# An earlier V load, bias copies on another queue and P V one head closer, in attention followed by a feed-forward block

## The chip, the cores and the metric

One Trainium2 chip, one core. Time is device time in microseconds of one launch. Each time is the median of several executions; the profile is one execution of its own.

## The reference, cut to what matters

```python
scores = q @ k^T / sqrt(64)                       # 8 batches x 8 heads, 576 positions
bias   = -(cum[..., :, None] - cum[..., None, :]) # cum = cumsum(max(s, 0))
scores = where(causal, -1e9, scores + minimum(bias, 0))
attn   = softmax(scores)
x      = (attn @ v).transpose(0, 2, 1, 3).reshape(4608, 512)
out    = (silu(x @ w_gate) * (x @ w_val)) @ w_out # 512 -> 1536 -> 512, float32
```

## The kernel before, in words

Attention runs head by head, 64 heads (`bh`), eight to a batch. Heads are grouped in sixteen blocks of four (`hb`). For a block, k and q are loaded in float32 (`load_one`, L112), cast to bfloat16 (`cast_one`, L191 and L193), transposed on TensorE (`pe_transpose`, L224; later blocks through a DMA) and copied into `KQ[hb % 2]` (`pe_out`, L237 and L239). The bias is not added by an engine: four rows of `KQ` beside the 64 of a head hold the cumulated s, as high and low parts (`HL`), so that the score product adds it. `aug(hb, ...)` (L178) copies these rows with four small DMAs, one for each head of the block, on the queues that it is given. `KQ[1]` needs memsets first, one of them at L505.

For one head `score_piece` makes the scores in four chunks (L268), ScalarE takes the exponential into `pt` (L276), and GpSimd masks the first and the last chunk (L280, L285). `av_piece` (L301) multiplies `pt` with V; V has 65 columns, the last all ones, so the row sums come along. `av_out` (L316, L317) divides by them on VectorE and leaves a bfloat16 tile `ot` for two heads; `x_pe` (L333) transposes that tile for the feed-forward part.

V of a batch is loaded in five chunks of up to 128 positions (`load_v`, L129, on SyncE's queue), into one buffer, in runs of 64 floats, and cast chunk by chunk (`cast_v`, L136). The first V is cast on GpSimd within the second head. Feed-forward weights are loaded and cast by DMAs that GpSimd issues (`w_load`, L250).

`attn_items` sets the order of the attention's work by a count `kk`. In the first batch P V of a head stands `lag` = 3 heads behind its scores, later 1. Where the first batch ends, `kk` runs on for four counts without scores, and then the second batch starts. `ffn_items` makes one tile of 512 rows: twelve times a gate product (`pg`, L453), a tanh, a value product (`pv`, L466) and two VectorE operations, and then the output products (`py`, L477). The main loop first runs `attn_items` to the end of the first batch (`start`) and then mixes it into the feed-forward items by `lo` and `hi`. Each engine and each queue works in the order in which its instructions were written. PSUM: three banks for scores (`scp`), one for P V (`avp`), four shared by transposes and feed-forward (`mp`).

Order of SyncE's queue at the start: s, k and q of blocks 0 and 1, bias copies of block 1, the first V, bias copies of block 2, k and q of block 2; then, behind the first batch's last scores, bias copies of block 3, the second V, k and q of blocks 3 and 4.

Of the kernel before, what the change touches and what calls it, by code (L numbers as in the profile page):

```python
# [12 lines left out]
FP32 = mybir.dt.float32  # L13
# [6 lines left out]
def kernel(  # L20
# [11 lines left out]
    nc = tc.nc  # L32
    PSUM = bass.MemoryType.PSUM

    B, H, S, D = q.shape
    NT, DM = out.shape
    DF = moe_w_gate.shape[1]
    BH = B * H
    NCH = 5
# [24 lines left out]
    def pt_col(tj, bi):  # L64
        if tj == bi:
            return DIAG_OFF[tj]
        return OFF_OFF[tj] + 128 * (bi - tj - 1)
# [11 lines left out]
    avp = ctx.enter_context(tc.tile_pool(name="avp", bufs=1, space=PSUM))  # L79
    mp = ctx.enter_context(tc.tile_pool(name="mp", bufs=4, space=PSUM))  # L80
# [23 lines left out]
    with tc.manual_schedule():  # L104
# [3 lines left out]
        def load_one(hb, name, rs=(0, NR)):  # L108
            b, g = divmod(hb, 2)
            if rs[0] == 0:  # L110
                loaded[name, hb] = raw.tile([128, NR, J, D], FP32, tag="raw" + name, name="raw" + name)
            nc.sync.dma_start(  # L112
                loaded[name, hb][:, rs[0] : rs[1], :, :].rearrange("x r j d -> x r (j d)"),
                SRC[name][0][b, g * HB + 2 * rs[0] : g * HB + 2 * rs[1], :, :].rearrange(
                    "(r e) (p j) d -> (e p) r (j d)", e=2, j=J
                ),
            )

        def load_qk(hb):
            load_one(hb, "k")  # L120
            load_one(hb, "q")

        def load_v(b, cs):
            if 0 in cs:
                loaded["v", b] = raw.tile([128, NCH, H, D], FP32, tag="rawv", bufs=1, name="rawv")
            t = loaded["v", b]
            for c in cs:
                n = 128 if c < 4 else TAIL
                nc.sync.dma_start(  # L129
                    t[0:n, c, :, :],  # L130
                    v[b, :, c * 128 : c * 128 + n, :].rearrange("h p d -> p h d"),
                )
# [5 lines left out]
        nc.sync.dma_start(s_sb, s.rearrange("b h n -> (b h) n"))  # L138
        load_qk(0)
        load_qk(1)  # L140

        ONES2 = 1.0019378662109375
        NEGS2 = -1.0058441162109375

        def aug_rows(i, r):
            r0 = 64 * (1 - r)
            return KQ[i][r][r0 : r0 + 64, :, :].bitcast(FP32)
# [26 lines left out]
        def aug(hb, engs):  # L174
            for hh in range(HB):
                r, e = divmod(hh, 2)
                r0 = 64 * (1 - r)
                engs[hh].dma_start(  # L178
                    KQ[hb % 2][r][r0 : r0 + 4, :, e * S : (e + 1) * S],
                    HL[hb * HB + hh : hb * HB + hh + 1, :, :, :],  # L180
                )

        SP4 = [nc.sync] * 4
# [3 lines left out]
        def cast_one(hb, name, eng):  # L187
            cts[name, hb] = cp.tile([128, J, NR, D], BF16, tag="c" + name, bufs=2, name="c" + name)
            dst = cts[name, hb].rearrange("x j r d -> x r j d")
            if eng is nc.scalar:  # L190
                nc.scalar.copy(dst, loaded[name, hb])  # L191
            else:
                eng.tensor_copy(dst, loaded[name, hb])  # L193
# [25 lines left out]
        def pe_transpose(hb, name, g):  # L219
            j0, j1 = JG[g]  # L220
            ps = mp.tile([128, j1 - j0, 128], BF16, tag="m", name="tps")
            ct = cts[name, hb]
            for j in range(j0, j1):
                nc.tensor.transpose(  # L224
                    ps[:, j - j0, :], ct[:, j].rearrange("x r d -> x (r d)"), ident
                )
            tps[name, g] = ps

        def pe_out(hb, name, g, r, eng):
            j0, j1 = JG[g]  # L230
            kq = SRC[name][1]
            dst = KQ[hb % 2][r][64 * r : 64 * r + 64, kq, 0 : NR * S].rearrange(
                "a (x j) -> a x j", j=J
            )[:, :, j0:j1]
            srcp = tps[name, g][64 * r : 64 * r + 64].rearrange("a j x -> a x j")
            if eng is nc.scalar:
                nc.scalar.copy(dst, srcp)  # L237
            else:
                eng.tensor_copy(dst, srcp)  # L239
# [50 lines left out]
        avs = {}  # L290

        def av_piece(bh, bis):
            b, h = divmod(bh, H)
            if bis[0] == 0:
                avs[bh] = avp.tile([128, NCH * (D + 1)], FP32, tag="av", name="av")
            av = avs[bh]
            pt = pts[bh]
            for bi in bis:
                for tj in range(bi + 1):
                    c0 = pt_col(tj, bi)  # L300
                    nc.tensor.matmul(  # L301
                        av[:, bi * (D + 1) : (bi + 1) * (D + 1)],
                        pt[:, c0 : c0 + 128],
                        VT[b % 2][:, tj, h, :],
                        start=(tj == 0),
                        stop=(tj == bi),
                    )
# [91 lines left out]
                        cast_v(bn, 4, nc.gpsimd)  # L399

        def attn_items():
            for kk in range(BH + 6):
                first = kk < H + 4
                bh = kk if first else kk - 4
                lag = 3 if first else 1
                b_lo, b_hi = (0, H) if first else (H, BH)
                h, step = divmod(bh, HB)
                if not first and step == 0 and 2 <= h < NPE:
                    if h > 3:
                        aug(h, SP4)  # L410
                    cast_one(h, "k", nc.gpsimd)
                    cast_one(h, "q", nc.gpsimd)
                    yield kk + 0.01
                    yield kk + 0.02
                    for g in range(2):
                        for nm in ("k", "q"):
                            pe_transpose(h, nm, g)
                            pe_out(h, nm, g, 0, nc.vector)
                            pe_out(h, nm, g, 1, nc.scalar)
                            yield kk + 0.03 + 0.02 * g  # L420
                if first and bh == H:
                    aug(3, SP4)
                    load_v(1, range(5))
                    load_qk(3)
                    load_qk(4)
                if bh < b_hi:
                    for ci in range(4):
                        score_piece(bh, ci)
                        if ci == 1:
                            side(h, step)  # L430
                        yield kk + 0.1 + ci / 8
                x = bh - lag - 1
                if b_lo <= x < b_hi and x % 2 == 1:
                    x_pe(x // 2)
                    yield kk + 0.5
                p = bh - lag
                if b_lo <= p < b_hi:
                    av_piece(p, (0, 1, 2))
                    yield kk + 0.6
                    av_piece(p, (3,))  # L440
                    yield kk + 0.7
                    av_piece(p, (4,))
                    av_out(p)
                    yield kk + 0.8
# [46 lines left out]
        def init_vt(i):  # L491
            nc.gpsimd.memset(VT[i][:, :, :, D : D + 1], 1.0)
            nc.gpsimd.memset(VT[i][64:128, 4, :, 0:D], 0.0)

        cast_one(0, "k", nc.scalar)
        cast_one(0, "q", nc.vector)
        aug(0, [nc.gpsimd] * 4)
        for nm, eng in (("k", nc.scalar), ("q", nc.vector)):
# [3 lines left out]
        for nm, eng in (("k", nc.scalar), ("q", nc.vector)):  # L502
            for g in range(2):
                pe_out(0, nm, g, 1, eng)
        nc.vector.memset(aug_rows(1, 1)[:, 0, :], 0.0)  # L505
        aug(1, SP4)
        load_v(0, range(5))
        init_vt(0)
        cast_one(1, "k", nc.vector)
        cast_one(1, "q", nc.vector)  # L510

        at = attn_items()
        state = {"pos": -1.0}

        def pump(upto):
            while state["pos"] < upto:
                try:
                    state["pos"] = next(at)
                except StopIteration:
                    state["pos"] = 1e9  # L520

        LAG = 1.65
        start = H + 3.45
        pump(start)
        hook = {
            21: [lambda: load_qk(5)],
        }
        for tt in range(NTT):
            lo = start if tt == 0 else H * (tt + 1) + 4 + LAG
            hi = min(H * (tt + 2) + 4 + LAG, BH + 6)  # L530
            span = 36
            n0 = 6 if tt == 0 else 0
            n = 0
            for _ in ffn_items(tt):
                n += 1
                for f in hook.pop(n, ()):
                    f()
                pump(lo + (hi - lo) * min(1.0, max(0, n - n0) / (span - n0)))
# [31 lines left out]
```

## Time and profile before

| | us |
|---|---|
| median of 3 executions | 427.64 (427.57 to 428.98) |
| the profiled execution | 429.72 |
| its span, first to last instruction | 428.0 |
| TensorE busy in it | 387.8 (91%) |
| VectorE, ScalarE, GpSimd busy | 251.3, 212.1, 124.2 |

Busy shares are means over the whole span. The first tenth of the kernel is different from the rest: there the attention of the first batch runs alone, and the feed-forward part begins only after it.

### The profile page before, as it was taken

The numbers are of one execution on the slowest core, as the hardware profiler recorded it, in microseconds if no ns is written. First come the engines' busy times: TensorE is split into PE (matmuls) and PEld (weight loads), VectorE is DVE, ScalarE is ACT, GpSimd is POOL, SyncE is SP. The second block draws the span as 40 slices with busy tenths as digits, with TensorE's granted clock in tenths as the row PEclk, the third lists the DMA queues.
The fourth block names the chain that finished last, engine by engine and source line by source line (L and its number), as shares of the span: only waits on it lengthen the run. The fifth ranks groups of instructions, "written<-read, shape, count | busy, mean of one in ns | idle before, by whom it ended". The sixth has DMA issues, their size and how long they took to land.

```text
span 428.0 us, 7940 instructions
## 1 busy us (share of the span) xinstructions
PE 387.8 (91%) x3029; PEld 214.8 (50%) x3082; DVE 251.3 (59%) x494; ACT 212.1 (50%) x421; POOL 124.2 (29%) x220
## 2 busy tenths in 40 slices
PE   2618779798999999999999999999999999999996
PEld 1416435454555555555555555555555554444442
DVE  7804466544688358836873686369636751871760
ACT  7506156555665555556555655555545552322321
POOL 5528023363416231623252235223411110000000
PEclk9957689898999999999999999999999999999999
DMA  6599979636493579447836774573320001002002
GB/s 238 108 176 231 186 237 182 221 102 182 141 239 91 167 185 219 112 163 184 204 99 200 176 188 112 187 188 81 94 78 26 2 13 70 17 2 99 0 2 98
DMA packets 85255, 56.71 MB, mean 132 GB/s; under 512 B 65456, under 2 KB 69520, under 8 KB 85216
## 3 DMA queue, kind: packets, MB, share of 16 engines
q1 hardware_dynamic: 81408, 51.44, 42.9%
q0 software_dynamic: 3808, 4.76, 6.8%
q8 instruction: 24, 0.39, 0.4%
q14 instruction: 15, 0.12, 0.1%
HBM read 37.90 MB, written 15.93 MB: 126 GB/s over the span
## 4 chain that ended last, share of the span: by engine, by line
PE 87%; DMA 5%; DVE 4%; issue 1%; SPq 1%; ACT 1%; POOL 0%; ACTq 0%
PE pg L453 22%; PE py L477 22%; PE pv L466 22%; PE sc L268 10%; PE av L301 8%; DMA rawv<-in_v_dram 3%; PE xps L333 3%; DVE kq L239 3%; DMA rawq<-in_q_dram 1%; DVE ot L317 1%; ACT pt L276 1%; SPq L129 0%; PE tps L224 0%; DVE ht L471 0%; SPq L178 0%
## 5 line engine op out<-in xcount | busy, mean ns | idle before, releaser
L276 ACT ACTIVATE pt<-sc 128x512 bf16<-128x512 f32 (+1 forms) x256 | 117.4, 505 | 66.5 <-PE sc L268 53.8
L460 DVE SCALAR_TENSOR_TENSOR pp<-th,pg 128x512 bf16<-128x512 bf16 x108 | 74.2, 687 | 66.0 <-ACT th L458 65.5
L453 PE MATMUL pg<-xt,wg 128*128 128x512 bf16 x416 | 111.4, 384 | 1.3 <-issue 0.5
L466 PE MATMUL pv<-xt,wv 128*128 128x512 bf16 x411 | 110.5, 384 | 1.2 <-issue 0.2
L458 ACT ACTIVATE th<-pg 128x512 bf16<-128x512 f32 x108 | 64.5, 597 | 91.3 <-PE pg L453 91.3
L477 PE MATMUL py<-wo,ht 128*128 128x512 bf16 x416 | 103.9, 382 | 0.9
L268 PE MATMUL sc<-kq 128*128 128x128 bf16 (+4 forms) x576 | 77.8, 250 | 8.3 <-DVE kq L239 5.5
L280 POOL TENSOR_SCALAR_AFFINE_SELECT pt<-pt 128x512 bf16<-128x512 bf16 x64 | 42.5, 665 | 146.1 <-ACT pt L276 143.7
L471 DVE TENSOR_TENSOR ht<-pp,pv 128x512 bf16<-128x512 bf16 x108 | 73.9, 685 | 9.1 <-PE pv L466 1.5
L268 PEld LDWEIGHTS <-kq 128*128 128x128 bf16 x576 | 47.6, 102 | 44.3 <-issue 6.1
L301 PE MATMUL av<-vt,pt 128*128 128x65 bf16 x960 | 51.6, 197 | 12.1 <-POOL vt L136 9.3
L301 PEld LDWEIGHTS <-pt 128*128 128x128 bf16 x960 | 42.4, 100 | 30.9 <-issue 12.5
L453 PEld LDWEIGHTS <-wg 128*128 128x128 bf16 x432 | 38.7, 99 | 36.9 <-issue 1.9
L466 PEld LDWEIGHTS <-wv 128*128 128x128 bf16 x432 | 38.9, 99 | 35.9 <-issue 1.9
L477 PEld LDWEIGHTS <-ht 128*128 128x128 bf16 x432 | 38.3, 98 | 35.4 <-issue 0.6
L485 ACT ACTIVATE ysb<-py 128x512 f32<-128x512 f32 x36 | 21.5, 597 | 44.5 <-PE py L477 42.4
L316 DVE RECIPROCAL rc<-av 128x5 f32<-128x5 f32 x64 | 12.2, 191 | 47.7 <-PE av L301 47.5
L285 POOL TENSOR_SCALAR_AFFINE_SELECT pt<-pt 128x64 bf16<-128x64 bf16 x64 | 15.4, 240 | 66.5 <-ACT pt L276 64.8
L317 DVE TENSOR_TENSOR ot<-av,rc 128x320 bf16<-128x320 f32 x64 | 31.5, 492 | 2.2
L337 DVE COPY xt<-xps 128x64 bf16<-128x64 bf16 (+7 forms) x32 | 9.8, 305 | 35.2 <-PE xps L333 35.2
L136 POOL CAST vt<-rawv 128x512 bf16<-128x512 f32 (+1 forms) x40 | 25.9, 673 | 9.5 <-DMA rawv<-in_v_dram 9.5
L333 PE MATMUL xps<-ident,ot 128*128 128x128 bf16 (+1 forms) x160 | 17.1, 220 | 1.6 <-DVE ot L317 1.6
(44 smaller groups left out, 152.9 us busy)
## 6 DMA issues: line engine op xcount, KB each, us to landing
rawk<-in_k_dram SPq DMA_DIRECT2D x16, 576.0 KB
rawq<-in_q_dram SPq DMA_DIRECT2D x16, 576.0 KB
out_dram<-ysb SPq DMA_DIRECT2D x36, 256.0 KB
rawv<-in_v_dram SPq DMA_DIRECT2D x32, 256.0 KB
ks<-ck SPq DMA_DIRECT2D x11, 288.0 KB
qs<-cq SPq DMA_DIRECT2D x11, 288.0 KB
wg<-in_moe_w_gate_dram POOLq DMA_DIRECT2D x2, 768.0 KB, 8.3
wv<-in_moe_w_val_dram POOLq DMA_DIRECT2D x2, 768.0 KB, 9.4
```

The lines of the kernel that those rows point to most:

```text
L268: nc.tensor.matmul(sc[:, o : o + w], T[:, 0, e * S + 128 * tj : e * S + 128 * (tj + 1)], T[:, 1, e * S + lo : e * S + hi], start=True, sto ...
L276: nc.scalar.activation(pt[:, CHUNK_PT[ci] : CHUNK_PT[ci] + o], sc[:, 0:o], AF.Exp, scale=0.125)
L280: nc.gpsimd.affine_select(pt[:, 1088:1600], pt[:, 1088:1600], pattern=[[0, 4], [1, 128]], compare_op=ALU.is_ge, fill=zreg, base=0, channel ...
L301: nc.tensor.matmul(av[:, bi * (D + 1) : (bi + 1) * (D + 1)], pt[:, c0 : c0 + 128], VT[b % 2][:, tj, h, :], start=(tj == 0), stop=(tj == bi),)
L317: nc.vector.tensor_mul(ot[:, :, e * D : (e + 1) * D], av3[:, :, 0:D], rc[:, :, None].to_broadcast([128, NCH, D]),)
L333: nc.tensor.transpose(ps[:, c * 128 : c * 128 + n], ot[0:n, c, :], ident[0:n, 0:n])
L453: nc.tensor.matmul(pg, WG[j][:, c, f0 : f0 + 128], xt[:, c, :], start=(c == 0), stop=(c == 3),)
L458: nc.scalar.activation(th, pg, AF.Tanh, scale=0.5)
L460: nc.vector.scalar_tensor_tensor(pp, in0=th, scalar=1.0, in1=pg, op0=ALU.add, op1=ALU.mult)
L466: nc.tensor.matmul(pv, WV[j][:, c, f0 : f0 + 128], xt[:, c, :], start=(c == 0), stop=(c == 3),)
L471: nc.vector.tensor_mul(ht, pp, pv)
L477: nc.tensor.matmul(py, hts[ft][:, ts_ * 128 : (ts_ + 1) * 128], WO[ft // WKO][:, ft % WKO, :], start=(ft == 0), stop=(ft == NFT - 1),)
```

## The change

Five edits. The first V load is issued right behind k and q of block 1. The bias copies of block 1 move from SyncE's queue to GpSimd's, behind the two memsets of V's tile. The memset at L505 moves ahead of the first q cast. P V of the first batch runs two heads behind the scores, and all counts that follow from it are less by one. P V of the odd heads of the first batch takes its bank from the shared pool of four.

```diff
         load_qk(0)
         load_qk(1)
+        load_v(0, range(5))
...
             if bis[0] == 0:
-                avs[bh] = avp.tile([128, NCH * (D + 1)], FP32, tag="av", name="av")
+                if b == 0 and h % 2 == 1:
+                    avs[bh] = mp.tile([128, NCH * (D + 1)], FP32, tag="m", name="avm")
+                else:
+                    avs[bh] = avp.tile([128, NCH * (D + 1)], FP32, tag="av", name="av")
...
-            for kk in range(BH + 6):
-                first = kk < H + 4
-                bh = kk if first else kk - 4
-                lag = 3 if first else 1
+            for kk in range(BH + 5):
+                first = kk < H + 3
+                bh = kk if first else kk - 3
+                lag = 2 if first else 1
...
         cast_one(0, "k", nc.scalar)
+        nc.vector.memset(aug_rows(1, 1)[:, 0, :], 0.0)
         cast_one(0, "q", nc.vector)
...
-        nc.vector.memset(aug_rows(1, 1)[:, 0, :], 0.0)
-        aug(1, SP4)
-        load_v(0, range(5))
         init_vt(0)
+        aug(1, [nc.gpsimd] * 4)
...
-        start = H + 3.45
+        start = H + 2.45
...
-            lo = start if tt == 0 else H * (tt + 1) + 4 + LAG
-            hi = min(H * (tt + 2) + 4 + LAG, BH + 6)
+            lo = start if tt == 0 else H * (tt + 1) + 3 + LAG
+            hi = min(H * (tt + 2) + 3 + LAG, BH + 5)
```

## Rows read from the trace of the kernel before

**Rows 1.** Stretches: from:to, length, busy PE, PEld, DVE, ACT, POOL, clock, DMA, GB/s.
```profile
10.00:14.00 4.00, 1.36 (x10) 0.92 (x11) 3.81 (x7) 1.25 (x3) 2.99 (x4) 1.00 0.04 7
...
24.00:28.00 4.00, 0.00 (x0) 0.00 (x0) 0.00 (x0) 0.00 (x0) 0.00 (x0) 0.50 1.17 212
...
34.00:37.00 3.00, 3.00 (x33) 2.29 (x31) 1.25 (x5) 1.71 (x5) 2.87 (x7) 0.50 1.07 182
...
41.00:44.00 3.00, 1.52 (x34) 1.29 (x35) 1.52 (x5) 0.00 (x0) 2.52 (x4) 0.99 1.10 205
...
48.00:51.00 3.00, 2.91 (x8) 1.14 (x8) 1.00 (x2) 0.60 (x1) 0.00 (x0) 0.54 1.21 222
...
100.00:200.00 100.00, 97.65 (x820) 55.16 (x834) 63.14 (x130) 57.45 (x117) 34.11 (x58) 0.98 0.60 166
```

**Rows 2.** Chain of work that ended last: start us, us, what.
```profile
16.53 13.73 DMA rawv<-in_v_dram
...
30.31 1.18 POOL vt L136 x2
...
31.75 1.44 PE sc L268 x9
...
33.19 0.82 PE av L301 x15
...
48.09 1.49 PE pg L453 x3
```

**Rows 3.** Timeline of SyncE's queue: start us, us of issuing, what.
```profile
14.37 11.15 SPq L129 DMA_DIRECT2D rawv<-in_v_dram  x5
25.71 4.08 SPq L178 DMA_DIRECT2D kq<-HL  x4
...
40.59 11.74 SPq L129 DMA_DIRECT2D rawv<-in_v_dram  x5
52.43 0.56 SPq L112 DMA_DIRECT2D rawk<-in_k_dram  x1
```

**Rows 4.** Timeline of GpSimd: start us, us, what, idle time before and its end.
```profile
8.02 2.50 POOL L178 DMA_DIRECT2D kq<-HL  x4 [4.23 <-DVE kq L172]
...
12.34 2.42 POOL L280 TENSOR_SCALAR_AFFINE_SELECT pt<-pt 128x512 bf16<-128x512 bf16 x1 [0.95 <-ACT pt L276]
...
17.61 0.64 POOL L280 TENSOR_SCALAR_AFFINE_SELECT pt<-pt 128x512 bf16<-128x512 bf16 x1 [0.25 <-ACT pt L276]
...
18.98 0.63 POOL L136 CAST vt<-rawv 128x512 bf16<-128x512 f32 x1
...
30.31 1.17 POOL L136 CAST vt<-rawv 128x512 bf16<-128x512 f32 x2 [0.26 <-DMA rawv<-in_v_dram]
...
63.10 2.84 POOL L136 CAST vt<-rawv 128x512 bf16<-128x512 f32 x5
```

**Rows 5.** Timeline of VectorE.
```profile
7.20 0.42 DVE L172 MEMSET kq<- 64x64 uint32 x4
...
12.42 0.56 DVE L505 MEMSET kq<- 64x608 f32 x1 [0.16 <-issue]
...
13.52 0.74 DVE L193 CAST cq<-rawq 128x1152 bf16<-128x1152 f32 x1
14.40 6.34 DVE L239 COPY kq<-tps 64x640 bf16<-64x640 bf16 x8
```

**Rows 6.** Timelines of ScalarE (first row) and TensorE, before the first feed-forward product.
```profile
37.39 3.31 ACT L276 ACTIVATE pt<-sc 128x512 bf16<-128x512 f32 x8 [1.17 <-PE sc L268]
...
41.66 0.62 PE L301 MATMUL av<-vt,pt 128*128 128x65 bf16 x15 [0.91 <-DVE ot L317]
...
45.18 0.99 PE L301 MATMUL av<-vt,pt 128*128 128x65 bf16 x15 [0.90 <-DVE ot L317]
...
46.98 0.77 PE L333 MATMUL xps<-ident,ot 128*128 128x128 bf16 x5 [0.81 <-DVE ot L317]
```

**Rows 7.** All bias copies up to 110 us (tile HL), landing times where shown.
```profile
DMA to landing us min/median/max: 1.9/2.1/2.8
```

## The prediction, made before the change was run

> **What bounds the kernel now.** I read the table of stretches first: between 100 and 200 us TensorE is busy 97.65 of 100 us [rows 1], so the middle is TensorE's. Nothing that the change touches makes that part shorter, so a gain has to come from the part before it. The chain of work that ended last, in order of time, shows where: from 16.53 on it goes through one piece of 13.73 us that is the first V load, and only at 31.75 does TensorE follow again, with scores and P V, up to the first feed-forward product at 48.09 [rows 2]. I call that moment F. Between 24 and 28 us no compute engine does anything, the DMA engines are full at 212 GB/s and the granted clock is 0.50 [rows 1]. SyncE's timeline shows why V is so late: its five loads are issued from 14.37 on and the issuing takes 11.15 us, while the DMA engines had stood almost idle (share 0.04) from 10 to 14 us [rows 1, 3]. On GpSimd the first V cast starts at 18.98 and the last two run from 30.31 for 1.17 us [rows 4]. So F is set by: V complete (31.5), then P V and scores of what is left.
>
> **Part 1, V issued behind q/k.** The five loads now stand in SyncE's queue before anything waits there. In the rings they follow the four q/k loads, which are done at about 10 us (the DMA share afterwards is 0.04). The loads are 1.18 MB (576 x 512 x 4 bytes); at the 212 GB/s that V and weights together reach between 24 and 28 us [rows 1] that is 5.6 us, so V has landed by about 15.6. The casts are queued on GpSimd behind head 1's first mask (17.61, 0.64 us) and the second weight load; the first ran at 18.98 in the kernel before, with nothing late in front of it. There I expect it again, but now with all five chunks there: five casts take 2.84 us where nothing holds them (63.10), at most 5 x 0.63 = 3.1 [rows 4]. V is complete at about 22.0 instead of 31.5: **9.5 us earlier**. SyncE then issues the second half's operations earlier too; its next ones, the bias copies that stood at 25.71 behind V's issuing [rows 3], wait for scores of heads 0 to 3.
>
> **Part 2, the bias copies of heads 4 to 7 on GpSimd.** Four issues of 2.50 us together [rows 4] stand behind the two V memsets, so from about 11.4 to 13.9. Queued behind them: head 0's mask (it ran from 12.34 on), the first weight load, and through these the V casts. In the kernel before that mask took 2.42 us where others take 0.64 [rows 4], and it lay beside a memset and two casts of VectorE, the last of which started at 13.52 for 0.74 us [rows 5]; it ended 0.5 us after them. If the mask, now begun at 13.9, takes 0.64 to 0.9 us, the queue is back in step by 14.8 and the part costs nothing. The cover is the wait for head 0's last exp and head 1's first, which GpSimd had until 17.61. If the copies are stretched as the mask was, by 1.78 us once, most of it still lies in that cover. Bounds: 0 and +1.8; I take 0. The copies' data are wanted by head 4's scores, 10 us later.
>
> The Trainium skill bears on this, in "SBUF — State Buffer", section "SBUF: two separate sides": GpSimd and VectorE share a pair of ports, a VectorE operation in a two-port mode holds it whole, and a GpSimd-issued DMA cannot write its descriptors meanwhile (its example: 620 ns become 3100 ns). By that figure four copies would cost 4 x 2.48 = 9.9 us, an estimate from that page, and the gain would be nearly gone; but the same section has the block end with the VectorE operation, which is what the mask's end here shows.
>
> **Part 3, the memset moved ahead of q's cast.** It takes 0.56 us at 12.42 [rows 5]; VectorE ends its small memsets at 7.62 (7.20 + 0.42) and starts q's cast at about 7.75, so q's cast goes back by 0.4 us and head 0's first scores by about 0.2. In return the casts for heads 4 to 7 start up to 0.2 us earlier, and the eight copies behind them (from 14.40, 6.34 us) end at about 20.6 instead of 20.7. Net zero for F, since the copies are wanted at about 24. The bias copies of heads 0 to 3 are now in flight together with V's packets; they landed in 1.9 to 2.8 us [rows 7]. A microsecond more would delay head 0's first scores, which the casts of heads 4 to 7 hold up anyway (13 to 15 us). I take 0, bound +0.5.
>
> **Part 4, P V two heads late.** When V was complete, the scores of heads 0 to 3 were done; now those of 0 to 2. One head's scores more lie behind V: 1.44 us of TensorE at the lower clock [rows 2], or 3.31 / 2 = 1.66 us of ScalarE [rows 6] where ScalarE limits. **+1.4 to 1.7**, I take 1.5.
>
> **Part 5, two banks for P V.** Heads 5 and 7 no longer wait until the output of the head before is read out of the only bank: waits of 0.91 and 0.90 us [rows 6] go: **-1.8**. What comes next in line are the transposes of a pair, which still wait 0.81 us for the second head's output (46.98) [rows 6]. The odd heads' banks come from the pool of four that the transposes use; the feed-forward part begins on the same slot (16 tiles before it instead of 12).
>
> **The sum.** From V complete to F: before 48.1 - 31.5 = 16.6; after 16.6 + 1.5 - 1.8 = 16.3. F comes at 22.0 + 16.3 = 38.3, that is 9.8 us earlier. From F on every engine has the same order as before (start, lo and hi move by one with the count of heads), and TensorE is full, so the shift goes through to the end. The loads that the second half needs move too: its V is issued behind the bias copies that wait for head 7's scores, by about 33 instead of 40.59 [rows 3], takes 11.7 us at most, lands by 46 and is cast at 63.10 - 9.8 = 53 [rows 4]; k of heads 12 to 15 goes from 52.43 to about 45 [rows 3]. They move by 7.5 us and not by 9.8, and have that slack.
>
> The profiled execution took 429.72 us (span 428.0, 1.7 around it), 2.1 above the median 427.64. 429.72 - 9.8 = 419.9 on its scale, **417.8 us** on the median's.
>
> **The clock, both ends.** The granted clock fell after TensorE's idle stretch, was 0.50 from 24 to 28 and still from 34 to 37 (although TensorE was busy all 3 us), high again from 41 to 44, and 0.54 on the first feed-forward products [rows 1]. My sum takes the same share of low clock as before. If the idle stretch is too short now for a fall, a head costs ScalarE's 1.66 us instead of 1.44 + 0.82 + half of 0.77 = 2.6 us at the lower level [rows 2, 6], for about three heads: -2.8; and the 3 us of low clock at F save up to 1.3 more. If it is low all the way, the high stretch before F goes too, in which a P V took 0.62 us where it took 0.82 to 0.99 at the lower level, scores and transposes likewise [rows 2, 6]; for the some 4 us of work in it +2.
>
> **The rivals.**
> (a) The clock stays high: 417.8 - 4.0 = 413.8. For it: V's gap on TensorE shrinks from about 10 us to about 3. Against: those 3 us hold hardly any work, and after a stretch of P V alone (41 to 44, busy 1.52 of 3 us) the clock was low at F [rows 1]. Chance 0.12.
> (b) GpSimd's queue holds up V, because its DMA issues and masks are blocked beside VectorE. Each blocked operation costs 1.78 us (2.42 - 0.64 [rows 4]); four copies give 7.1 us, hence 424.9. Ahead of V complete stand 4 copies, 2 weight loads and 5 casts: if all 11 were stretched, V would be complete 10 us later than before and the time **437.4, slower than before**; it turns from gain to loss at the sixth (9.8 / 1.78 = 5.5). Against it: beside the copies from 14.40 on, the mask at 17.61 and the cast at 18.98 had their usual 0.64 and 0.63 us [rows 4, 5]. The page named in part 2 describes this rival. Chance 0.03 for the slower end, 0.05 for the part between.
> (c) Another load becomes the bound (the first feed-forward weights or the second half's V, k or q), as they move by less than F: half of the gain would be given back, 422.7. Against: 7 us of slack for V above. Chance 0.05.
> (d) The V load isn't earlier in effect, because its 256-byte packets get in front of q/k or of the bias copies: no change, 427.6. Against: they stand behind q/k in the same queue. Chance 0.03.
>
> **How the numbers follow.** My forecast, with its own range of 415.5 to 421.6 (low clock all the way +2.0 and GpSimd +1.8 above; part of the clock's gain below), has 0.72; (a) 0.12, (b) 0.08, (c) 0.05, (d) 0.03. The range 413.8 to 421.6 holds forecast and (a). A measurement of this kernel can tell some 0.5% (2.1 us) from no change. Faster by more: forecast, (a), (c) and half of (b)'s middle, together 0.92; within: 0.05; slower: 0.03.
>
> **What would show it.** The V casts without a gap from about 19 to 22 us; the first feed-forward product near 38; no wait of P V for the output of the head before; the rest of the chain as long as before (about 380 us). Wrong if GpSimd's first cast starts much after 20, if the first mask ends after 16, or if the distance from the first feed-forward product to the end grows by more than a microsecond.

## The result, and the profile after

The changed kernel took 414.50 us (median of 4, 413.56 to 416.77) against 427.61 (median of 4): ratio 0.9704, 95% interval 0.9647 to 0.9762. In a later group on another occasion the same kernel took 416.26 (4 runs) against 426.98, ratio 0.9739 (0.9706 to 0.9772). So the gain is 11 to 13 us; 417.8 had been forecast, with a range of 413.8 to 421.6. The profiled execution after took 413.63 us, its span is 411.9.

The chain of work that ended last, kernel after (start us, us, what). [rows 2] showed the piece of 13.73 us that was V; it is gone, and the first feed-forward product F stands at 36.39 instead of 48.09. A new long piece has come: a bias copy (`kq<-HL`) of 5.28 us.

```profile
8.23 5.28 DMA kq<-HL
...
13.64 1.01 PE sc L269 x6
...
19.67 2.85 POOL vt L136 x5
...
22.78 1.33 PE sc L269 x9
24.11 0.82 PE avm L305 x15
...
36.39 0.99 PE pg L457 x4
```

SyncE's queue after, beside [rows 3]: V is issued from 3.64 on, its issuing still takes 9.51 us, but nothing waits behind it. The second half's V is issued at 32.80 instead of 40.59.

```profile
3.64 9.51 SPq L129 DMA_DIRECT2D rawv<-in_v_dram  x5
17.12 7.63 SPq L179 DMA_DIRECT2D kq<-HL  x4
...
32.80 11.48 SPq L129 DMA_DIRECT2D rawv<-in_v_dram  x4
```

GpSimd after, beside [rows 4]: eight bias copies, the first mask back at 0.63 us, and the five V casts in one piece from 19.67 to 22.5.

```profile
8.23 2.82 POOL L179 DMA_DIRECT2D kq<-HL  x4 [4.45 <-DVE HL L170]
...
11.87 2.61 POOL L179 DMA_DIRECT2D kq<-HL  x4
15.00 0.63 POOL L281 TENSOR_SCALAR_AFFINE_SELECT pt<-pt 128x512 bf16<-128x512 bf16 x1 [0.53 <-ACT pt L277]
...
19.67 2.84 POOL L136 CAST vt<-rawv 128x512 bf16<-128x512 f32 x5
```

Stretches after (columns as in [rows 1]). The granted clock is 0.81 and 0.62 in the two stretches around V's completion and 1.00 from there through F, where the kernel before had 0.50 from 34 to 37 and 0.54 at F.

```profile
20.00:23.00 3.00, 1.85 (x22) 1.32 (x21) 1.71 (x4) 1.09 (x3) 3.00 (x7) 0.81 1.16 210
23.00:26.00 3.00, 2.81 (x30) 2.15 (x29) 1.19 (x4) 2.23 (x6) 2.08 (x5) 0.62 1.11 202
...
35.00:38.00 3.00, 2.14 (x13) 1.11 (x14) 1.29 (x5) 0.59 (x1) 0.74 (x1) 1.00 1.16 209
```

The span is 16.1 us shorter in these two profiles. F accounts for 11.7. The rest, 4.4 us, lies behind F, where the program is the same: 428.0 - 48.1 = 379.9 before, 411.9 - 36.4 = 375.5 after. The stretch from F to 110 us tells why. First before, then after:

```profile
48.09:110.00 61.91, 53.80 (x432) 30.45 (x439) 33.68 (x65) 35.04 (x68) 22.63 (x37) 0.90 0.66 181
```

```profile
36.39:110.00 73.61, 66.18 (x578) 37.93 (x579) 45.72 (x89) 44.18 (x87) 26.55 (x45) 0.98 0.84 212
```

A mean clock of 0.90 over 61.91 us is 0.10 / 0.5 x 61.91 = 12.4 us at the lower level; 0.98 over 73.61 us is 2.9 us. Half of the difference is 4.7 us, about the 4.4 that are missing. This reading is tried on every kernel below.

### The profile page after: what moved, and what is told of

It is laid out like the page before. It is cut to its first block, busy times and chain, and to the rows that moved or that the text cites. A ratio compares the mean times of both kernels' runs of the same rounds, so it can differ in the third digit from the quotient of the medians.

```text
span 411.9 us, 7992 instructions
## 1 busy us (share of the span) xinstructions
PE 383.5 (93%) x3082; PEld 211.9 (51%) x3082; DVE 251.0 (61%) x494; ACT 212.0 (51%) x421; POOL 125.2 (30%) x224
## 4 chain that ended last, share of the span: by engine, by line
PE 90%; DVE 4%; DMA 2%; ACT 1%; POOL 1%; issue 1%; ACTq 0%; POOLq 0%
PE pg L457 23%; PE py L481 23%; PE pv L470 22%; PE sc L269 11%; PE av L305 7%; PE xps L337 3%; DVE kq L240 2%; DMA kq<-HL 1%; ACT pt L277 1%; DMA s_sb<-in_s_dram 1%; POOL vt L136 1%; PE tps L225 1%; DVE ot L321 1%; DVE c L167 0%; PE avm L305 0%
## 5 line engine op out<-in xcount | busy, mean ns | idle before, releaser
L481 PE MATMUL py<-wo,ht 128*128 128x512 bf16 x432 | 105.7, 379 | 0.0
L269 PE MATMUL sc<-kq 128*128 128x128 bf16 (+4 forms) x576 | 76.4, 247 | 10.4 <-DVE kq L240 5.5
L281 POOL TENSOR_SCALAR_AFFINE_SELECT pt<-pt 128x512 bf16<-128x512 bf16 x64 | 40.8, 637 | 140.0 <-ACT pt L277 137.7
L305 PEld LDWEIGHTS <-pt 128*128 128x128 bf16 x960 | 41.2, 98 | 20.9 <-issue 3.0
L305 PE MATMUL av<-vt,pt 128*128 128x65 bf16 x900 | 47.4, 194 | 2.0 <-POOL vt L136 0.9
L321 DVE TENSOR_TENSOR ot<-av,rc 128x320 bf16<-128x320 f32 x60 | 29.5, 491 | 2.1
L240 DVE COPY kq<-tps 64x640 bf16<-64x640 bf16 (+1 forms) x24 | 17.5, 762 | 2.3 <-PE tps L225 2.1
```

The lines of the kernel that those rows point to most:

```text
L269: nc.tensor.matmul(sc[:, o : o + w], T[:, 0, e * S + 128 * tj : e * S + 128 * (tj + 1)], T[:, 1, e * S + lo : e * S + hi], start=True, sto ...
L281: nc.gpsimd.affine_select(pt[:, 1088:1600], pt[:, 1088:1600], pattern=[[0, 4], [1, 128]], compare_op=ALU.is_ge, fill=zreg, base=0, channel ...
L305: nc.tensor.matmul(av[:, bi * (D + 1) : (bi + 1) * (D + 1)], pt[:, c0 : c0 + 128], VT[b % 2][:, tj, h, :], start=(tj == 0), stop=(tj == bi),)
L321: nc.vector.tensor_mul(ot[:, :, e * D : (e + 1) * D], av3[:, :, 0:D], rc[:, :, None].to_broadcast([128, NCH, D]),)
L481: nc.tensor.matmul(py, hts[ft][:, ts_ * 128 : (ts_ + 1) * 128], WO[ft // WKO][:, ft % WKO, :], start=(ft == 0), stop=(ft == NFT - 1),)
```

## The experiments

The theory: V's arrival is most of the gain, the second bank pays about what the shorter lag costs, and the granted clock is the rest. Rivals: the parts need each other; the bias copies on GpSimd cost or pay; the clock is no part of it. F is again the start of the first feed-forward product.

**V early alone**, on the kernel before.

```diff
         load_qk(1)
+        load_v(0, range(5))
...
         aug(1, SP4)
-        load_v(0, range(5))
```

> The kernel before with one edit: the first V load right behind the q/k loads; P V still three heads late, one bank, bias copies of heads 4 to 7 on SyncE's queue, memset late. Let F be the start of the first feed-forward product (48.1 before, 36.4 after). Theory 1 (V's arrival is the gain): the V casts run without a gap from about 19.5 to 22.5, F is at 38 to 39, and the time is 9 to 11 us under the kernel before. Theory 2 (the gain needs the shorter lag and the second bank with it): F stays above 42 and the time is at most 6 us under it.

Measured: 418.63 us against 426.77, ratio 0.9815 (0.9778 to 0.9852). F is at 37.85, so this one edit moves F by 10.2 of the 11.7 us. The theory holds for F; in time it brings 8.1, less than the 9 that were expected at least. The spans of the two profiles differ by 9.2 (428.0 and 418.8), 1.0 less than F: the clock is low at F, and the table behind the experiments puts that 1.0 on it. Its stretch from 36 to 40:

```profile
36.00:40.00 4.00, 3.19 (x16) 1.39 (x14) 1.21 (x4) 0.29 (x1) 0.00 (x0) 0.50 1.18 200
```

**V at its old place in the program**, the rest as after.

```diff
         load_qk(1)
-        load_v(0, range(5))
...
         init_vt(0)
+        load_v(0, range(5))
         aug(1, [nc.gpsimd] * 4)
```

> The kernel after, but the V load written where it stood before, right ahead of the bias copies, which stay on GpSimd's queue. Theory 1 (what held V was the bias copies ahead of it on SyncE's queue, not its place in the program): SyncE's queue has nothing else there, so V is issued at about 3.6 us as in the kernel after, F at 36.4 and the time is that of the kernel after within 1.5 us. Theory 2 (the place counts): V is issued at 10 us or later, and F is later by up to 2 us.

Measured: 416.59 us (414.32 to 418.35), F at 36.13. SyncE's queue, first row its V load:

```profile
3.63 9.06 SPq L129 DMA_DIRECT2D rawv<-in_v_dram  x5
```

V is issued at 3.63 as in the kernel after. What had held it were the bias copies ahead of it on SyncE's queue, which waited for the late memset; moving either of the two is enough. The median lies 2.1 above the first group's of the kernel after, more than the 1.5 that were allowed, and 0.3 above the second group's, with F 0.3 us earlier: the table behind the experiments puts the difference on the clock.

**Bias copies of heads 4 to 7 ahead of V on SyncE's queue**, the early memset kept.

```diff
         load_qk(1)
-        load_v(0, range(5))
...
-        init_vt(0)
-        aug(1, [nc.gpsimd] * 4)
+        aug(1, SP4)
+        load_v(0, range(5))
+        init_vt(0)
```

> The kernel after, but the bias copies of heads 4 to 7 on SyncE's queue again, ahead of V; all else as after, the early memset too, so that they don't wait for it. In the kernel after the bias copy of head 0 landed 5.3 us after its issue, beside V's packets (up to 2.8 in the kernel before). Theory 1 (V's packets hold that copy up): V is issued from about 10 us on, head 0's first scores start at 11 to 12 instead of 13.6, the casts at 19.0 instead of 19.7, V is complete at 22 all the same, and F is 0.3 to 0.8 us earlier than in the kernel after. Theory 2 (the copy is slow for another reason): scores start at 13.6 again and F is the same or later. If V were not there by 19, F would be later by 2 us or more.

Measured: 415.26 us (ratio 0.9737, 0.9707 to 0.9767), F at 36.52. The bias copies of GpSimd's queue landed in 2.2 to 3.3 us instead of 3.1 to 5.3:

```profile
DMA to landing us min/median/max: 2.2/2.8/3.3
```

Head 0's scores start at 11.35 instead of 13.64. So V's packets do hold those copies up; the run with V alone says the same, where one edit took them from 1.9 to 2.8 us [rows 7] to 4.4 to 6.0. But F gains nothing. Of the 2.3 us won at the scores, 0.13 reach the V casts (19.54 instead of 19.67), as TensorE now waits for VectorE's casts of heads 4 to 7. The first of them began beside GpSimd's mask, and they took 1.22 and 0.94 us instead of the 0.76 and 0.75 of the kernel after:

```profile
12.71 0.63 POOL L280 TENSOR_SCALAR_AFFINE_SELECT pt<-pt 128x512 bf16<-128x512 bf16 x1 [1.01 <-ACT pt L276]
...
12.74 1.22 DVE L193 CAST ck<-rawk 128x1152 bf16<-128x1152 f32 x1
13.88 0.94 DVE L193 CAST cq<-rawq 128x1152 bf16<-128x1152 f32 x1
```

And V, issued from 10.26, is now last: GpSimd waits 0.20 us for its last chunk.

```profile
22.02 0.61 POOL L136 CAST vt<-rawv 64x512 bf16<-64x512 f32 x1 [0.20 <-DMA rawv<-in_v_dram]
```

Theory 1 was right on the cause and wrong on F.

**P V three heads late.** The counts of `attn_items` and the main loop as before, the rest as after (`lag = 3`, `H + 4`, `kk - 4`, `start = H + 3.45`).

> The kernel after, but P V three heads late as before. Theory 1 (my step: the shorter lag costs a head's scores behind V): head 3's scores run in TensorE's gap before V is complete, F is 0.8 to 1.5 us earlier than in the kernel after (35 to 35.6), the time 0.5 to 1.5 us lower. Theory 2 (the shorter lag saves a P V behind the last scores and so pays for itself): F is the same or up to 1 us later.

Measured: F at 35.11, 1.3 us earlier, as theory 1 had it. The time is 414.80 (413.16 to 415.81), the same as after. The 1.3 us were gone at once: the clock was low at F.

```profile
35.00:38.00 3.00, 3.00 (x9) 1.14 (x9) 0.92 (x3) 0.60 (x1) 0.00 (x0) 0.55 1.17 200
```

In this profile the transposes that follow the first eight feed-forward items start at 43.26, and in that of the kernel after at 43.26 too.

The lag also changes the clock ahead of that. With three heads of lag TensorE has head 3's scores to do before V is complete, and the clock stays up there. Kernel after, then this one:

```profile
20.00:26.00 6.00, 4.66 (x49) 3.47 (x48) 2.90 (x7) 3.32 (x9) 5.08 (x11) 0.72 1.14 206
```

```profile
20.00:26.00 6.00, 4.79 (x64) 3.22 (x62) 3.05 (x7) 5.36 (x14) 5.99 (x13) 1.00 1.16 217
```

It is so in every profile with an early V: with two heads of lag the clock falls between 21 and 24.1 us, unless that gap is filled (below), and with three it does not. So part of the 1.3 us is the clock's; the run with lag 3 and products says how much.

**One bank for P V**, the rest as after (the `if` around `avm` taken out).

> The kernel after, but all heads' P V in the one bank as before. Theory 1 (my step, two waits of 0.9 us): F (36.4 in the kernel after) comes at 37.3 to 38.2, as P V of heads 5 and 7 waits for the output of the head before again. Theory 2 (the waits are hidden or turn into the transposes' wait): F within 0.4 us of 36.4.

Measured: F at 37.54, 1.15 us later, at the low end of theory 1. But the time is 420.57 (417.79 to 420.86), ratio to before 0.9831 (0.9779 to 0.9883): 4 to 6 us above the kernel after. TensorE's timeline before F:

```profile
31.54 0.62 PE L302 MATMUL av<-vt,pt 128*128 128x65 bf16 x15
...
34.97 0.98 PE L302 MATMUL av<-vt,pt 128*128 128x65 bf16 x15 [0.91 <-DVE ot L318]
```

P V of head 5 (31.54) has no wait even with one bank, since with two heads of lag it comes right behind head 7's scores; only head 7's wait of 0.91 is left. And the clock is low at F:

```profile
38.00:41.00 3.00, 3.00 (x9) 1.08 (x8) 0.79 (x2) 0.60 (x1) 0.00 (x0) 0.50 1.21 197
```

**The memset late**, the rest as after.

> The kernel after, but the memset of the bias rows where it stood before, so that the bias copies of heads 4 to 7, now on GpSimd's queue, wait for it there. Theory 1 (the move matters once GpSimd waits for it): GpSimd stands until about 13, its first copy of the four starts at 13 instead of 11.9, they end at 15.6 or later, head 0's mask and the weight load follow late, the V casts start at 19.7 to 20.7, F at 36.4 to 37.4. Theory 2 (a VectorE matter only): q's cast 0.5 us earlier, and F 0.2 to 0.5 us earlier than in the kernel after, unless V's packets hold the scores up anyway (then no change).

Measured: F at 36.33, 414.61 us: no difference. GpSimd's four copies took 4.09 us instead of 2.61, from 11.37 to 15.46, the first mask started at 15.52 instead of 15.00, and the V casts at 19.82 instead of 19.67. The cover named in part 2 of the prediction hid it. The wait for the memset isn't what took the time: the memset ended at 12.92. It is the issue of the second copy, which took 2.35 us and ended 0.10 us behind VectorE's second cast:

```profile
11.95 2.35 POOL L179 DMA_DIRECT2D kq<-HL  x1
...
12.36 0.56 DVE L509 MEMSET kq<- 64x608 f32 x1 [0.16 <-issue]
12.85 0.69 DVE L194 CAST ck<-rawk 128x1152 bf16<-128x1152 f32 x1
13.46 0.74 DVE L194 CAST cq<-rawq 128x1152 bf16<-128x1152 f32 x1
```

Neither theory is borne out. What shows, in this one profile, is what rival (b) is made of: an issue held beside VectorE, for 1.76 us more than its usual 0.59, the size that part 2 gave as its bound.

**The gap before V's completion filled** with products that nobody reads, on the kernel after.

```diff
             for bi in bis:
+                if bh == 0:
+                    if bi == 0:
+                        fill.append(mp.tile([128, 512], FP32, tag="m", name="fill"))
+                    nc.tensor.matmul(
+                        fill[0], KQ[0][0][:, 0, 0:128], KQ[0][0][:, 1, 0:512],
+                        start=True, stop=True,
+                    )
```

> The kernel after with five products of 512 columns added, whose result isn't used: one ahead of each of the five parts of head 0's P V, in the gap in which TensorE waits for the V casts. In the kernel after, the clock fell at 22.2 for 3.4 us. Theory 1 (low clock behind the gap costs time, as in rival a): with the gap filled the clock stays high from its rise at about 19 until the end of the scores, F is 0.7 to 1.5 us earlier (34.9 to 35.7). Theory 2 (ScalarE limits there): F within 0.4 us of 36.4, whatever the clock.

Measured: the clock stays at 1.00 between 23 and 26, F is at 35.49, 0.9 us earlier. So the low clock behind the gap did cost time at F, less than the 1.7 us that 3.4 us at half speed would make, as ScalarE limits part of it (it is busy all 3 us from 23 to 26). The time is 415.33 (413.17 to 416.76), no better.

**The long gap of the kernel before filled**, V late as before: eight products ahead of the second and twenty ahead of the third part of head 0's P V.

> The kernel before with 28 products of 512 columns added, whose result isn't used: 8 ahead of the second and 20 ahead of the third part of head 0's P V, in TensorE's long wait for V. V stays late, only the clock is changed. Theory 1 (of the gain at F, 11.7 us, some 3 are the clock behind the gap and the rest is V's arrival): V complete at 31.5 again, the clock high from there, scores of heads 4 to 7 limited by ScalarE, F at 44.5 to 46.5 (48.1 before), the time 1.5 to 3.5 us under the kernel before. Theory 2 (the clock is no part of it): F within 0.6 us of 48.1.

Measured: F at 48.21, 426.80 us against 427.51, ratio 0.999 (0.9962 to 1.0017). Theory 2's number, but it decides nothing: the products ended at 28.8, V was complete at 32.2, and the clock fell again at 32.9. From V complete to F it was at the lower level for 8.3 of 16.0 us, against 9.6 of 16.6 in the kernel before, so the edit changed little of what it was to change. It shows only that filling that gap in this way doesn't replace V's arrival.

**The stalls filled**, after the profiles had shown the same places in all kernels: four products ahead of the last two transposes before F, nine behind each of the three groups of q/k transposes (heads 8 to 19). Three kernels had them, and the kernel after ran beside them unchanged.

```diff
+        def fill(n):
+            f = scp.tile([128, 512], FP32, tag="sc", name="fill")
+            for _ in range(n):
+                nc.tensor.matmul(
+                    f, WG[0][:, 0, 0:128], WG[0][:, 1, 0:512], start=True, stop=True
+                )
...
                             pe_out(h, nm, g, 1, nc.scalar)
+                            if g == 1 and nm == "q":
+                                fill(9)
...
+                    if first and bh >= H:
+                        fill(4)
                     x_pe(x // 2)
```

> The kernel after, unchanged, beside the three below on one chip. Theory (the low-clock stretches behind F come by chance): F at 36.4 within 0.4 us again, but low stretches of 3.4 us at other places than in the first profile, and times spread over 413.5 to 418.

Measured: 416.26 us (415.06 to 416.73). F is at 37.42, a microsecond later than in the first profile and out of the 0.4 that I gave it: here the clock, once fallen, stayed low for twice as long.

```profile
23.00:26.00 3.00, 3.00 (x32) 2.39 (x32) 1.35 (x4) 1.89 (x5) 2.41 (x6) 0.50 1.16 211
26.00:29.00 3.00, 2.91 (x33) 2.14 (x32) 1.24 (x5) 1.92 (x5) 1.62 (x4) 0.63 0.99 176
```

> The kernel after with products of 512 columns added whose result isn't used: four ahead of the last two transposes before F, and nine behind each of the three groups of q/k transposes of heads 8 to 19, where TensorE waits 2.3 us for the copies out of PSUM (44 to 47 us in the kernel after). Theory 1 (what differs from run to run behind F is the clock that falls at these three stalls, 1.7 us each): no low stretch between 26 us and the end, F to the end shorter than 375.5 us by 1 to 2, times 411.5 to 414 with a spread under 1.5 us. Theory 2 (the added products cost what they save): no gain or a loss of up to 1 us a stall.

Measured: 413.62 us (413.01 to 414.20), 2.6 under the kernel after of this group, spread 1.2 instead of 1.7 to 3.2. No low clock from F to 110:

```profile
36.94:110.00 73.06, 70.37 (x605) 39.78 (x606) 45.73 (x89) 44.07 (x87) 26.46 (x45) 1.00 0.87 213
```

F to the end takes 375.1 us, 0.4 less than in the first profile of the kernel after and not 1 to 2 less: the clock's time is saved, and the products cost some of it (they end 0.36 us ahead of what TensorE waits for, but delay a little at each place). Of its other executions one has a mean clock of 0.989 over the whole span, the profiled one 0.996, so the products don't keep every fall away.

> As the one before, with P V three heads late. With that lag F came at 35.1 without added products, but the clock was low there. Theory 1 (lag 3 is worth 1.3 us once the clock holds): F at 34.8 to 35.5, no low stretch behind it, the time 0.7 to 1.5 us under the run before: 410.5 to 413. Theory 2: the same time as the run before, within 0.5 us.

Measured: **411.88 us** (411.37 to 412.56), ratio to before 0.9642 (0.9610 to 0.9673). F at 35.79, 1.15 us earlier than with lag 2, although V is complete 0.8 us later (23.59 against 22.82). This is the fastest version that was run, 4.4 us under the kernel after of the same group. The clock is at 1.00 from 20 to 40 and on to 110.

```profile
35.79:110.00 74.21, 71.52 (x613) 40.36 (x614) 46.75 (x92) 44.51 (x88) 26.52 (x45) 1.00 0.91 219
```

With lag 2 and products the clock was still low from 24.0 to 27.4. The fair pair is lag 2 with the gap filled and this run, both at full clock from V complete to F:

```profile
22.43:35.49 13.06, 10.07 (x173) 7.59 (x172) 6.95 (x22) 8.32 (x20) 9.46 (x20) 1.00 1.11 238
```

```profile
23.59:35.79 12.20, 10.99 (x171) 7.54 (x171) 6.86 (x22) 6.63 (x17) 10.29 (x21) 1.00 1.13 257
```

At one clock the third head of lag is worth 0.9 us.

> As the second of this group (two heads late, products added) with one bank for P V. Without added products one bank cost 6 us in the median, of which F explained 1.2. Theory 1 (the rest is the clock, low from 35.3 to 42.2 there and at three stalls): with the clock held, one bank costs 0.8 to 2.0 us against the run with two banks. Theory 2 (one bank costs in another way, such as later loads): 4 us or more against it again.

Measured: 414.64 us (413.61 to 415.08), F at 37.70. One bank costs 1.0 us here and had cost 4 to 6 without the products. Theory 1: most of what the second bank brings comes by the clock.

## Where the time is, in one table

L is the time at the lower clock between F and 110 us, (1 - mean clock) / 0.5 x length, from the row of that stretch in each profile (the clock is given to two decimals, so L is good to 0.7 us).

| kernel | F | mean clock, F to 110 | L | F to the end | less L / 2 | median |
|---|---|---|---|---|---|---|
| before | 48.09 | 0.90 | 12.4 | 379.9 | 373.7 | 427.61 |
| after | 36.39 | 0.98 | 2.9 | 375.5 | 374.0 | 414.50 |
| after, again | 37.42 | 0.95 | 7.3 | 377.3 | 373.6 | 416.26 |
| V early alone | 37.85 | 0.90 | 14.4 | 380.9 | 373.7 | 418.63 |
| V at its old place | 36.13 | 0.91 | 13.3 | 380.5 | 373.8 | 416.59 |
| bias copies ahead of V | 36.52 | 0.95 | 7.3 | 376.7 | 373.0 | 415.26 |
| lag 3 | 35.11 | 0.94 | 9.0 | 378.8 | 374.3 | 414.80 |
| one bank | 37.54 | 0.90 | 14.5 | 381.2 | 373.9 | 420.57 |
| memset late | 36.33 | 0.98 | 2.9 | 375.4 | 373.9 | 414.61 |
| gap filled | 35.49 | 0.93 | 10.4 | 379.1 | 373.9 | 415.33 |
| before, gap filled | 48.21 | 0.93 | 8.7 | 377.9 | 373.6 | 426.80 |
| stalls filled | 36.94 | 1.00 | 0 | 375.1 | 375.1 | 413.62 |
| stalls filled, lag 3 | 35.79 | 1.00 | 0 | 375.0 | 375.0 | 411.88 |
| stalls filled, one bank | 37.70 | 1.00 | 0 | 375.1 | 375.1 | 414.64 |

In the eleven profiles without products at the stalls the last column but one is 373.0 to 374.3, whatever the change: the span is F + 373.8 + L / 2. With the products it is 375.0 to 375.1, so they cost 1.3 us. The low stretches behind F are 3.4 us each and begin while TensorE waits for the copies of a group of q/k transposes or up to 1.4 us after, or run on from before F. This is the wait in the kernel after:

```profile
44.75 0.38 PE L225 MATMUL tps<-ident,cq 128*128 128x128 bf16 x4 [0.41 <-DVE ht L475]
47.43 0.60 PE L269 MATMUL sc<-kq 128*128 128x128 bf16 x6 [2.30 <-DVE kq L240]
```

There are three such waits in every profile without these products (two of 2.3 us, the third in pieces of 0.65 and 0.87), and not each brings a fall: none at this one in the first profile after, one in the second. "After" and "V at its old place" run the same order on SyncE and TensorE and had L of 2.9, 7.3 and 13.3. Which of the waits meets a fall therefore isn't a property of the kernel alone, as far as these runs show; what sets it for a given execution wasn't tried. The kernel has a part in it: of the one-bank kernel's four executions three lie at a mean clock of 0.973 or 0.974, and the kernel after is never under 0.983.

The spans of single executions say the same. The eight of the kernel after have spans of 411.9 to 415.1 us at mean clocks of 0.991 to 0.983. Taking half of (1 - mean clock) / 0.5 x span off each leaves 407.5 to 408.4: a spread of 3.2 us becomes one of 0.9.

## Why the prediction was right, and where its numbers came from something else

The first median, 414.50, lies under the forecast's own range (415.5 to 421.6) and is covered by rival (a)'s end of the wider one; the second, 416.26, lies in both. The sum below shows how far the clock, and with it chance, had a part in that.

- **Part 1** (V 9.5 us earlier): V complete at 22.5, 22.0 forecast. The casts ran without a gap from 19.67. V alone moved F by 10.2 us. Right.
- **Part 2** (copies on GpSimd cost nothing): four copies took 2.61 us at 11.87, while VectorE's two casts ran at 12.95 and 13.62 for 0.76 and 0.75 us. The rule of "SBUF — State Buffer" in the Trainium skill, section "SBUF: two separate sides", would have held each until VectorE's operation ended, and the last two were: they ended 0.09 and 0.10 us behind the two casts, in 0.77 and 0.67 us where the first two took 0.59. That is 0.3 us together, not the 9.9 of the estimate. The mask that had taken 2.42 us took 0.63; it now ran behind VectorE's casts. So rival (b)'s times are out, but its mechanism is there: with the memset late it took 1.76 us once, and the cover hid it.

```profile
13.03 0.77 POOL L179 DMA_DIRECT2D kq<-HL  x1
13.80 0.67 POOL L179 DMA_DIRECT2D kq<-HL  x1
```

- **Part 3** (nothing for the memset): right, by the late memset's run. But I gave the bias copies beside V's packets at most 0.5 us. They landed in 3.1 to 5.3 us instead of 1.9 to 2.8 [rows 7], and head 0's scores began at 13.64 instead of 11.2. The casts of heads 4 to 7 hid most of that, as the prediction said. The V casts began 0.7 us later than before (19.67 instead of 18.98), but that isn't the bias copies' doing alone: with scores from 11.35 on they began at 19.54.
- **Part 4** (+1.5): lag 3 gave 1.3 at F, and 1.15 with the products. Right in kind, and the number in part by luck: a head's scores behind V cost 0.9 us at one clock, and the rest is the fall between 21 and 24 us, which comes with the shorter lag and stands in no term. In the time it was hidden by the clock, and is seen only with the products: 413.62 against 411.88.
- **Part 5** (-1.8): mis-sized at F. It was 1.15, or 0.8 with the products: of the two waits that I read from [rows 6] one was gone already by the shorter lag. The two terms can't be added as read from a trace with three heads of lag. In time the part was worth 4 to 6 us, through the clock.
- **The sum**: from V complete to F 16.3 forecast, 13.9 measured. The step that failed is "the same share of low clock as before". From V complete to F, kernel before and kernel after:

```profile
31.49:48.09 16.60, 12.32 (x163) 9.42 (x164) 7.36 (x24) 6.69 (x16) 10.36 (x20) 0.71 1.06 210
```

```profile
22.51:36.39 13.88, 10.97 (x172) 8.53 (x172) 6.96 (x22) 8.38 (x20) 10.51 (x20) 0.90 1.09 237
```

  A mean clock of 0.71 is 9.6 us at the lower level, and 0.90 is 2.8. Parts 4 and 5 as measured (+0.9 and -0.8) come to +0.1, so 16.6 + 0.1 - 13.9 = 2.8 us are left for the clock. Half of the difference of 6.8 us is 3.4, the most that it can give; at the rate of the filled gap (0.9 for 3.4 us) it would be 1.8. Rival (a), at 0.12, gave 413.8 for a clock that stays high; it didn't stay high but came back early, so the truth lies between forecast and (a). The second profile, F at 37.42, lies nearer to the forecast's 38.3.
- **The rest of the chain "as long as before"**: 375.5 and 377.3 instead of 379.9. I had taken F to the end as fixed; it moves by L / 2, 1.8 us between the two profiles of the kernel after and up to 7 us between all of them.

Loads of the second half kept up: its V was issued at 32.80 (33 forecast) and cast at 50.25 without a wait, so rival (c) is out, and (d) by V's row.

## What to carry to other kernels

A load that sits behind a waiting operation in its queue is late by that wait; look at what stands ahead of it in the queue, not at where it stands in the program. Where TensorE is the bound, the time from a fixed point to the end can be checked against the granted clock first: here one sum, F + 373.8 + L / 2, separates what an edit did from what the clock did, and two edits (one bank, lag 3) look quite different in time and at F. Products whose result isn't used, put where TensorE waits anyway, kept the clock up from F on in all three profiles, for 1.3 us of their own. The times were steadier too: they spread over 1.2 to 1.5 us in these three groups, and over 1.7 to 4.0 in the nine groups of four with an early V and no such products.

## What the runs showed of the hardware that was not expected

- Small copies issued by GpSimd landed in 3.1 to 5.3 us beside V's packets of 256 bytes on SyncE's queue, in 1.9 to 2.8 us without them.
- A DMA issue on GpSimd that met VectorE's casts from float32 to bfloat16 ended 0.1 us behind a cast three times (0.77, 0.67 and 2.35 us instead of 0.59). Where a mask on GpSimd began just ahead of a cast, the mask kept its 0.63 us and the cast took 1.22.
- Two executions of one program differ by 2.8 us (1.0 up to F, 1.8 behind it) through the number and place of 3.4-us stretches at the lower clock.
- At the start the clock column reads 1.00 although TensorE runs at the lower level: five transposes take 0.72 us at 14.46 in the kernel after and 0.44 at 43.26, and the next group starts 0.52 us later there and 0.27 here, nearly half. Up to 16 us at least the column should not be believed; durations should.

```profile
14.46 0.72 PE L225 MATMUL tps<-ident,ck 128*128 128x128 bf16 x5
14.98 0.74 PE L225 MATMUL tps<-ident,cq 128*128 128x128 bf16 x5
...
43.26 0.44 PE L225 MATMUL tps<-ident,ck 128*128 128x128 bf16 x5
43.53 0.44 PE L225 MATMUL tps<-ident,cq 128*128 128x128 bf16 x5
```
